# Batch tails in pairs, one more transpose by DMA, and a new order, in an attention and mixing kernel

## The chip, the cores and the metric

The kernel runs on one core of a Trainium2 chip. The metric is the device time of one launch in microseconds, the median of the runs. Engines are named as in the profile: PE multiplies matrices, PEld loads its weights, DVE is the vector engine, ACT the scalar engine, POOL the GpSimd engine, SP the engine whose queue issues every DMA here.

## The reference

There are 8 batches of 8 heads, 576 positions and 64 channels a head. Attention has a pooled part and a local part, and its result x (576 x 512 per batch) goes through a mixing layer:

```
out_d = softmax(q_d k_d^T / 8) v_d          # q, k, v averaged over groups of 4 positions
x = repeat(out_d, 4) + softmax(mask(q k^T / 8)) v   # mask: |i - j| < 4
theta = x @ w_theta
y = w_tok_r @ (x * cos(theta)) + w_tok_i @ (x * sin(theta))
u = x + y
out = u + max(u @ w_ch, 0)
```

## The kernel before, in words

The work of each batch is a set of generators, one for each kind of step, and each step puts a handful of instructions on the engines. One string, `ORDER` (L80), names the steps of all eight batches by letters, in the order in which they are issued. `pin` (L698) ties each instruction to the one before it on its engine, so that every engine follows this order strictly, and so does SP's queue of DMAs. A step that waits therefore holds up everything behind it on its engine. Data dependences between engines are semaphores.

The steps by letter: L and v load q, k and v; C and w cast them to bf16 (ACT for q of batch 0, otherwise POOL); A turns q and k (L324 to L343: PE transposes into PSUM, or for batches 6 and 7 DMA transposes issued by q at L296; ACT then copies in two halves, and DVE pools over four positions). B pools v (L350 to L359). Q makes the pooled scores and their exp (two steps, L382 to L409). S makes the local scores in five chunks with an exp on ACT (L438) and, but for batch 0, two band masks on POOL (L445, L447). N and V are the pooled and local outputs (L464, L502). T adds the two into x, transposed (L541, L545); for batches 6 and 7, t has turned it by DMA (L304) and POOL adds. H makes the angles and their cosine and sine (five steps, L562 to L580). Z multiplies them with x in the other layout: for batches 6 and 7 that comes from one DMA transpose (step x, L312), for the rest from PE (L604), 16 transposes a batch. X is the token mixing (L623 for 512 positions in four steps, L629 for the last 64, the tail), and DVE adds x (L624, L631). u turns u by DMA (L639 for the main part, L641 for the tail). R multiplies by w_ch (L653, and L661 for the tail), O adds on DVE (L675) and stores (L681, and L684 for the tail). W, c, l, g, h and D prepare weights and warm PE up.

S, N, Q and V, and the PE form of A, share two PSUM tiles of two banks, "w2", taken in turn. B, T, H, X, R, Z and the last step of N share four of one bank, "w1". The output tile `osb` has four buffers. ACT holds one table at a time: exp for Q and S, sine for H.

The tail of a batch has 64 positions. In R it fills both halves of the 128 partitions: at L661 eight matmuls of 256 columns, four for each half of the output channels, with the same 64 weights columns of u. In the store, the two halves go out as two DMAs of 64 KB in runs of 128 channels:

```
lhsT=uB[:, dc, :],
rhs=wch[:, dc, :].rearrange("p (j e d) -> p e j d", j=2, e=2)[:, hf],
```

Of the kernel before, what the change touches and what calls it, by code (L numbers as in the profile page):

```python
# [10 lines left out]
BF16 = mybir.dt.bfloat16  # L11
AF = mybir.ActivationFunctionType
ALU = mybir.AluOpType
AX = mybir.AxisListType

P = 128
B = 8
H = 8
S = 576
# [22 lines left out]
HALF = 64  # L42
MAIN = 512
# [4 lines left out]
def kernel(  # L48
# [11 lines left out]
    nc = tc.nc  # L60
# [5 lines left out]
    moep = ctx.enter_context(tc.tile_pool(name="moep", bufs=2))  # L66
# [9 lines left out]
    def w1(name, dt=FP32):  # L76
        return ps1.tile([P, 512 if dt == FP32 else 1024], dt, tag="w1" + next(turn1), name=name)


    ORDER = (  # L80
        "LKLLLLLKKCLCCAvCCLvCDwvvvKLCAACwwwwLASCLSVQQCBlLLLLLVSlllllNvlCCCCNlvvvACNVCcScwcvTlTTccllcwAASlHVVH"
        "wwwDTTcAHZHZcHSZcccSDDhLLLzBcCSCWQDVWWLghLLLLCWCCvQvWWLNCNCCWWSWvvLvZNVVXwwwvAAvhwhTXTAALXSwSLLLLXQQ"
        "TBCCVgLggHCuLLVTvHNTVHHZNCCHCCCSwzZZZARRvvvSwOROALSXOLLAAXLLwSwwLvCCCCSCCCCRSNVOXVVXQVTTTAABwSXuTLLA"
        "vvwuvQRvvLLSTSHONNHVLLXuZZANHCLwHwwLVVHRQRRCCCCOzvLLLBOOCCSSTZTCvvRwOTLZSQHVHNVTXTAAXLLACACwCHHwCLCq"
        "LwwqNVHXSZNVXZZvvzSLLCCQCLqXVZLqQvRvwBvOVTVuTTLXTAwASSCHCCHCHNNXqvLwwTwuVXLVLAAHHXqSSZXRQROzONZSCCQC"
        "TCZBSVqROqvvvvZTSSROTVHVRHOTNNTXAAHVHHVwwwwwXAtAXSSzXXSSZZNZVuRuuRRROOQQtOOBRVRVttROtTTTOZOSTNXVRTuN"
        "RRxSSOOOHHVVXtttVHZHZZHNVzZXXttXuXTTXXHTHTTRxROOZHHRuROOHZRZZzOXXXXXXXRuRRRuuOORRuOOROROOORROO"
    )

    staged = {}  # L90
# [86 lines left out]
    for i in range(2):  # L177
        t = const.tile([P, 4, 5, KP], BF16, name=f"kdP{i}")
# [4 lines left out]
    for i in range(2):  # L183
        t = const.tile([P, 4, 5 * 120], BF16, name=f"kT{i}")
# [4 lines left out]
    for i in range(2):  # L189
        t = const.tile([P, NCH, H, 66], BF16, name=f"v_w{i}")  # L190
# [4 lines left out]
    for c in range(NCH):  # L195
        t = const.tile([P, DM], BF16, name=f"tmp{c}")
# [4 lines left out]
    for i in range(2):  # L201
        t = const.tile([P, 2, H, 66], BF16, name=f"vd{i}")
# [12 lines left out]
    wch = wpool.tile([P, 4, DM], BF16, name="wch")  # L215
# [69 lines left out]
    parts, turned = {}, {}  # L285


    DMA_QK, DMA_X, DMA_Z = (6, 7), (6, 7), (6, 7)

    def turn_qk(b):  # L290

# [229 lines left out]
    def parted(t):  # L521

        return (t[:, 0:4 * MAIN].rearrange("p (e t) -> p e t", e=4),
                t[:, 4 * MAIN:4 * S].rearrange("p (e t) -> p e t", e=4))
# [85 lines left out]
            yield  # L610


    uTs, urs = {}, {}

    def mix(b):

        (xA, xB), z = parted(xTs[b]), zs.pop(b)
        uT = uTs[b] = moep.tile([P, 4 * S], BF16, tag="uT", name=f"uT{b}")
        uA, uB = parted(uT)
        for dc in range(4):  # L620
            ps = w1(f"psu{dc}_{b}")
            for j in range(9):
                nc.tensor.matmul(out=ps, lhsT=z[:, j, P * dc:P * dc + P], rhs=WT[:, j, 0:MAIN], start=(j == 0), stop=(j == 8))  # L623
            nc.vector.tensor_tensor(out=uA[:, dc, :], in0=ps, in1=xA[:, dc, :], op=ALU.add)  # L624
            yield
        ps = w1(f"psut_{b}")[:, 0:4 * HALF].rearrange("p (e t) -> p e t", e=4)
        for dc in range(4):
            for j in range(9):
                nc.tensor.matmul(out=ps[:, dc, :], lhsT=z[:, j, P * dc:P * dc + P], rhs=WT[:, j, MAIN:S],  # L629
                                 start=(j == 0), stop=(j == 8))  # L630
        nc.vector.tensor_tensor(out=uB, in0=ps, in1=xB, op=ALU.add)  # L631
        yield

    def u_turn(b):

        ur = moep.tile([P, 16, P], BF16, tag="ur", name=f"ur{b}")
        utr = moep.tile([P, 2, P], BF16, tag="utr", name=f"utr{b}")
        urs[b] = ur, utr
        nc.sync.dma_start_transpose(out=ur, in_=uTs[b][:, 0:4 * MAIN])  # L639
        yield  # L640
        nc.sync.dma_start_transpose(out=utr, in_=uTs[b][:, 4 * MAIN:4 * S])  # L641
        yield

    rels = {}

    def channels(b):

        uA, uB = parted(uTs[b])
        for c in range(5):
            psr = rels[b, c] = w1(f"psr{c}_{b}")  # L650
            if c < 4:
                for dc in range(4):
                    nc.tensor.matmul(  # L653
                        out=psr, lhsT=uA[:, dc, P * c:P * c + P], rhs=wch[:, dc, :],
                        start=(dc == 0), stop=(dc == 3),
                    )
            else:

                for dc in range(4):
                    for hf in range(2):  # L660
                        nc.tensor.matmul(  # L661
                            out=psr[64 * hf:64 * hf + 64, 0:256], lhsT=uB[:, dc, :],
                            rhs=wch[:, dc, :].rearrange("p (j e d) -> p e j d", j=2, e=2)[:, hf],
                            start=(dc == 0), stop=(dc == 3),
                        )
            yield

    def store(b):

        ur, utr = urs.pop(b)  # L670
        for c in range(5):
            psr = rels.pop((b, c))
            osb = moep.tile([P, DM], FP32, tag="osb", bufs=4, name=f"osb{c}_{b}")
            n = 4 if c < 4 else 2
            nc.vector.scalar_tensor_tensor(  # L675
                out=osb[:, 0:P * n].rearrange("p (e d) -> p e d", d=P),
                in0=psr[:, 0:P * n].rearrange("p (e d) -> p e d", d=P), scalar=0.0,
                in1=ur[:, c:16:4, :] if c < 4 else utr, op0=ALU.max, op1=ALU.add,
            )
            if c < 4:  # L680
                nc.sync.dma_start(out=out[b, P * c:P * c + P, :], in_=osb)  # L681
            else:
                for hf in range(2):
                    nc.sync.dma_start(  # L684
                        out=out[b, 512:576, :].rearrange("t (j e d) -> e t j d", j=2, e=2)[hf],
                        in_=osb[64 * hf:64 * hf + 64, 0:2 * P].rearrange("p (j d) -> p j d", j=2),
                    )
            yield

    last = {}
# [13 lines left out]
    def batches(steps):  # L709
        for b in range(B):  # L710
            yield from steps(b)

    sequences = dict(L=batches(load), v=batches(load_v), C=batches(cast), w=batches(cast_v), A=batches(turns), B=batches(pooled_v), Q=batches(scores), S=batches(band_scores), N=batches(pooled_out), q=batches(turn_qk), t=batches(turn_x), x=batches(turn_z),
                     V=batches(outputs), T=batches(transposes), H=batches(phases), Z=batches(modulate),
                     K=constants(), z=batches(z_turn), u=batches(u_turn), X=batches(mix), R=batches(channels), O=batches(store),
                     l=weight_loads(), c=weight_casts(), h=channel_loads(), g=channel_casts(), W=weight_turns(), D=warm_up())
    pin()
# [35 lines left out]
```

## Time and profile before

| what | before |
|---|---|
| median of 6 runs | 247.75 us (245.97 to 248.63) |
| the profiled execution, its time | 248.63 us |
| its span | 246.9 us |
| PE, DVE, ACT, POOL busy | 221.4, 185.8, 166.7, 161.4 us |
| mean granted clock of PE | 0.986 |
| L623, token mixing | 65.2 us of PE |
| L653 and L661, channel mixing, main and tail | 30.8 and 5.0 us of PE |
| L604, transposes of x | 96 matmuls |
| L675, tail additions | 8 of 417 ns |
| DMA issues L641, L684, L312 | 8, 16, 2 |

The span runs from the first to the last instruction; the time of an execution includes what lies around it. Busy times of an engine join overlapping instructions. A line of the page's fifth part gives the time of a group, the mean of one instruction, and how long the engine stood idle before them, with what ended the wait. The chain of waits follows back from the last instruction to what released each step. "L623" is line 623 of the kernel.

### The profile page before, as it was taken

How to read it: one execution, taken by the hardware profiler on the slowest of the kernel's cores; microseconds unless marked ns; L12 is line 12 of the kernel's file. 1: busy time of each engine (PE TensorE's matmuls, PEld its weight loads, DVE VectorE, ACT ScalarE, POOL GpSimd, SP SyncE). 2: the span in 40 equal slices, each digit the busy share in tenths (PEclk: the TensorE clock that was granted, in tenths of full speed). 3: DMA queues.
4: the chain of work that ended last, by engine and by line, in shares of the span. 5: the costliest groups of instructions: out<-in, count | busy, mean ns of one | idle time of the engine just before them, and what ended most of it. 6: DMA issues, size and time to landing. Idle time of an engine off the chain costs nothing. (4 is left out here: it accounts for less than half of the span.)

```text
span 246.9 us, 6575 instructions
## 1 busy us (share of the span) xinstructions
PE 221.4 (90%) x2569; PEld 134.1 (54%) x2602; DVE 185.8 (75%) x345; ACT 166.7 (68%) x248; POOL 161.4 (65%) x223
## 2 busy tenths in 40 slices
PE   0767799999999999999999998999699999999990
PEld 0434465765666566656666555655455655455540
DVE  5274979779879898887989977997787776256462
ACT  3586799766998479998878999899924390250000
POOL 4367466998999999989858764996295952400000
PEclk9999999999999999999999999999979999999997
DMA  6999999999999997999999999399869584957496
GB/s 197 302 252 377 314 188 322 316 231 231 317 229 286 310 213 137 281 249 295 234 202 214 264 196 269 50 195 201 120 155 156 138 210 93 169 182 87 91 262 202
DMA packets 100511, 53.94 MB, mean 218 GB/s; under 512 B 83968, under 2 KB 86016, under 8 KB 100480
## 3 DMA queue, kind: packets, MB, share of 16 engines
q1 hardware_dynamic: 100480, 53.53, 91.8%
q8 instruction: 20, 0.33, 0.6%
q14 instruction: 11, 0.09, 0.1%
HBM read 33.59 MB, written 9.44 MB: 174 GB/s over the span
## 5 line engine op out<-in xcount | busy, mean ns | idle before, releaser
L623 PE MATMUL psu<-WT,z 128*128 128x512 bf16 x273 | 65.2, 379 | 1.3 <-ACT cs L568 0.5
L445 POOL TENSOR_SCALAR_AFFINE_SELECT pm<-pm 128x1024 bf16<-128x1024 bf16 (+1 forms) x35 | 36.7, 1049 | 18.7 <-ACT pm L438 18.7
L438 ACT ACTIVATE pm<-psS 128x1024 bf16<-128x1024 f32 (+1 forms) x40 | 37.7, 979 | 11.6 <-PE psS L430 10.7
L623 PEld LDWEIGHTS <-z 128*128 128x128 bf16 x288 | 26.8, 98 | 29.2 <-issue 0.8
L447 POOL TENSOR_SCALAR_AFFINE_SELECT pm<-pm 128x1024 bf16<-128x1024 bf16 (+1 forms) x35 | 36.6, 1046 | 2.4
L624 DVE TENSOR_TENSOR uT<-psu,xT 128x512 bf16<-128x512 f32 x32 | 21.8, 686 | 12.8 <-PE psu L623 12.6
L562 PE MATMUL psth<-wth,xT 128*128 128x512 bf16 x120 | 30.9, 379 | 0.5
L653 PE MATMUL psr<-wch,uT 128*128 128x512 bf16 x119 | 30.8, 385 | 0.6 <-issue 0.2
L131 POOL CAST v_w<-st_v 128x512 bf16<-128x512 f32 (+1 forms) x40 | 24.0, 615 | 10.0 <-DMA st_v<-in_v_dram 10.0
L567 ACT ACTIVATE cs<-psth,pihc 128x512 bf16<-128x512 f32 x32 | 22.2, 695 | 11.8 <-PE psth L562 11.3
L511 DVE TENSOR_TENSOR tmp<-psloc,rl 120x512 bf16<-120x512 f32 (+2 forms) x40 | 27.6, 690 | 1.4
L342 DVE TENSOR_REDUCE qdT<-qT 128x288 bf16<-128x1152 bf16 x16 | 21.5, 1347 | 9.4 <-ACT qT L334 9.4
L675 DVE SCALAR_TENSOR_TENSOR osb<-psr,ur 128x512 f32<-128x512 f32 x32 | 21.5, 686 | 7.7 <-PE psr L653 6.7
L342 DVE TENSOR_REDUCE kdP<-kT 128x300 bf16<-128x1200 bf16 x16 | 22.3, 1396 | 5.5 <-ACT kT L334 5.5
L124 POOL CAST k_tm<-st_k 128x576 bf16<-128x576 f32 x32 | 21.7, 677 | 5.3 <-DMA st_k<-in_k_dram 4.8
L334 ACT COPY qT<-pstr 128x576 bf16<-128x576 bf16 x24 | 14.2, 646 | 9.2 <-PE pstr L332 9.2
L545 DVE TENSOR_TENSOR xT<-xTps,xdT 128x480 bf16<-128x480 bf16 (+3 forms) x36 | 18.7, 547 | 1.5 <-PE xTps L541 1.3
L124 POOL CAST q_tm<-st_q 128x576 bf16<-128x576 f32 x28 | 18.6, 664 | 1.6 <-PE pstr L332 1.0
L568 ACT ACTIVATE cs<-psth 128x512 bf16<-128x512 f32 x32 | 19.3, 604 | 0.0
L653 PEld LDWEIGHTS <-uT 128*128 128x128 bf16 x128 | 11.6, 99 | 12.5 <-issue 1.3
L430 PE MATMUL psS<-qT,kT 64*128 64x128 bf16 (+1 forms) x320 | 14.9, 217 | 3.2 <-ACT pm L438 2.2
L502 PEld LDWEIGHTS <-pm 128*128 128x128 bf16 (+1 forms) x320 | 14.8, 104 | 4.8 <-issue 0.5
(92 smaller groups left out, 389.1 us busy)
## 6 DMA issues: line engine op xcount, KB each, us to landing
st_q<-in_q_dram SPq DMA_DIRECT2D x32, 288.0 KB, 5.2
st_k<-in_k_dram SPq DMA_DIRECT2D x32, 288.0 KB, 4.9
st_v<-in_v_dram SPq DMA_DIRECT2D x32, 256.0 KB, 5.2
out_dram<-osb SPq DMA_DIRECT2D x32, 256.0 KB, 3.1
st_v<-in_v_dram SPq DMA_DIRECT2D x8, 192.0 KB, 4.9
tok<-in_moe_w_tok_r_dram SPq DMA_DIRECT2D x4, 288.0 KB, 7.2
tok<-in_moe_w_tok_i_dram SPq DMA_DIRECT2D x4, 288.0 KB, 5.3
th<-in_moe_w_theta_dram SPq DMA_DIRECT2D x2, 512.0 KB, 7.0
```

The costliest lines, as they stand in the source:

```text
L124: eng[i](out=dst[:, hh // 2, :, hh % 2, :], in_=staged.pop((b, f"{'qk'[i]}{hh}")).rearrange("p (r d) -> p r d", d=D))
L131: gp(out=v_ws[b % 2][0:KW[c], c, :, 0:D], in_=staged.pop((b, f"v{c}"))[0:KW[c], 0:DM].rearrange("p (h d) -> p h d", d=D))
L342: nc.vector.tensor_reduce(out=dst, in_=src, axis=AX.X, op=ALU.add)
L438: nc.scalar.activation(out=pv, in_=ps[0:kw].rearrange("p e (j w) -> p (e j) w", w=P)[:, :, 0:qn], func=AF.Exp, scale=SCL,)
L445: nc.gpsimd.affine_select(out=pv, in_=pv, compare_op=ALU.is_ge, fill=0.0, base=off, pattern=[[0, 8], [-1, qn]], channel_multiplier=1)
L447: nc.gpsimd.affine_select(out=pv, in_=pv, compare_op=ALU.is_ge, fill=0.0, base=6 - off, pattern=[[0, 8], [1, qn]], channel_multiplier=-1)
L511: nc.vector.tensor_tensor(out=tmp[0:cnt].rearrange("p (e j d) -> p e j d", e=2, j=4), in0=pv[0:cnt, :, :, 0:D], in1=rl[0:cnt].unsqueeze(3) ...
L562: nc.tensor.matmul(out=th, lhsT=xA[:, dc, P * c:P * c + P], rhs=wth[:, dc, :], start=(dc == 0), stop=(dc == 3),)
L567: nc.scalar.activation(out=cs[:, 0, :], in_=th, func=AF.Sin, bias=pihc, scale=1.0)
L623: nc.tensor.matmul(out=ps, lhsT=z[:, j, P * dc:P * dc + P], rhs=WT[:, j, 0:MAIN], start=(j == 0), stop=(j == 8))
L624: nc.vector.tensor_tensor(out=uA[:, dc, :], in0=ps, in1=xA[:, dc, :], op=ALU.add)
L653: nc.tensor.matmul(out=psr, lhsT=uA[:, dc, P * c:P * c + P], rhs=wch[:, dc, :], start=(dc == 0), stop=(dc == 3),)
```

## The change

Three things are changed. First, u of the tail is kept for two batches side by side (tile `uB`, one for each pair), so that R treats the 128 tail positions of a pair as one more chunk of four matmuls of 512 columns. This is done with the odd batch: an even batch now has four R and four O steps, an odd one five. The tails of a pair are turned by one DMA transpose of four blocks, added by one DVE instruction of 512 columns and stored by two DMAs of 64 rows of 2 KB. Second, batch 5 takes x for Z by a DMA transpose as batches 6 and 7 do. Third, `ORDER` is another string throughout; the tail's steps are fewer in it (O and R 36 for 40, u 12 for 16, x 3 for 2), and the other letters are as many as before.

The ends of the two strings, in the letters above (batch.step, from the last main mixing of batch 7 on):

```
before: X7.3 X7.4 R6.0 u6.0 R6.1 R6.2 R6.3 u6.1 u7.0 O6.0 O6.1 R6.4 R7.0 u7.1 O6.2 O6.3 R7.1 O6.4 R7.2 O7.0 O7.1 O7.2 R7.3 R7.4 O7.3 O7.4
after:  X7.3 R6.0 R6.1 R6.2 u7.0 R6.3 O6.0 O6.1 O6.2 O6.3 X7.4 u7.1 R7.0 R7.1 O7.0 R7.2 R7.3 O7.1 R7.4 O7.2 O7.3 O7.4
```

The stretch from the cosines of batch 5 on, without the steps that load or cast:

```
before: H5.0 V5.4 R2.4 H5.1 O2.4 T5.3 N6.0 N6.1 T5.4 X4.0 A7.0 A7.1 H5.2 V6.0 H5.3 H5.4 V6.1 X4.1 A7.2 t6.0 A7.3 X4.2 S6.3 S6.4 z5.0 X4.3 X4.4 S7.0
after:  H5.0 H5.1 N6.0 N6.1 T5.3 X4.0 T5.4 V6.0 V6.1 q7.3 A7.0 A7.1 x5.0 H5.2 H5.3 X4.1 A7.2 H5.4 A7.3 u3.0 S6.3 S6.4 X4.2 X4.3 z5.0 Z5.0 u3.1 R3.0 u4.0 Q7.0
```

The diff, without the string:

```diff
-    DMA_QK, DMA_X, DMA_Z = (6, 7), (6, 7), (6, 7)
+    DMA_QK, DMA_X, DMA_Z = (6,7),(6,7),(5,6,7)
...
-        uT = uTs[b] = moep.tile([P, 4 * S], BF16, tag="uT", name=f"uT{b}")
-        uA, uB = parted(uT)
+        uT = uTs[b] = moep.tile([P, 4 * MAIN], BF16, tag="uT", name=f"uT{b}")
+        uA = uT.rearrange("p (e t) -> p e t", e=4)
+        if b % 2 == 0:
+            uBs[b // 2] = moep.tile([P, 4, 2, HALF], BF16, tag="uB", name=f"uB{b // 2}")
+        uB = uBs[b // 2][:, :, b % 2, :]
...
-        nc.sync.dma_start_transpose(out=ur, in_=uTs[b][:, 0:4 * MAIN])
-        yield
-        nc.sync.dma_start_transpose(out=utr, in_=uTs[b][:, 4 * MAIN:4 * S])
-        yield
+        ur = urs[b] = moep.tile([P, 16, P], BF16, tag="ur", name=f"ur{b}")
+        nc.sync.dma_start_transpose(out=ur, in_=uTs[b])
+        yield
+        if b % 2:
+            utr = utrs[b // 2] = moep.tile([P, 4, P], BF16, tag="utr", name=f"utr{b // 2}")
+            nc.sync.dma_start_transpose(out=utr, in_=uBs[b // 2].rearrange("p e i t -> p (e i t)"))
+            yield
...
-        for c in range(5):
+        for c in range(4 + b % 2):
             psr = rels[b, c] = w1(f"psr{c}_{b}")
...
+            for dc in range(4):
+                nc.tensor.matmul(
+                    out=psr, lhsT=uA[:, dc, P * c:P * c + P] if c < 4 else uBs[b // 2][:, dc],
+                    rhs=wch[:, dc, :], start=(dc == 0), stop=(dc == 3),
+                )
             yield
...
             nc.vector.scalar_tensor_tensor(
-                out=osb[:, 0:P * n].rearrange("p (e d) -> p e d", d=P),
-                in0=psr[:, 0:P * n].rearrange("p (e d) -> p e d", d=P), scalar=0.0,
-                in1=ur[:, c:16:4, :] if c < 4 else utr, op0=ALU.max, op1=ALU.add,
+                out=osb.rearrange("p (e d) -> p e d", d=P),
+                in0=psr.rearrange("p (e d) -> p e d", d=P), scalar=0.0,
+                in1=ur[:, c:16:4, :] if c < 4 else utrs.pop(b // 2), op0=ALU.max, op1=ALU.add,
             )
...
-                for hf in range(2):
-                    nc.sync.dma_start(
-                        out=out[b, 512:576, :].rearrange("t (j e d) -> e t j d", j=2, e=2)[hf],
-                        in_=osb[64 * hf:64 * hf + 64, 0:2 * P].rearrange("p (j d) -> p j d", j=2),
-                    )
+                for i in range(2):
+                    nc.sync.dma_start(out=out[b - 1 + i, 512:576, :], in_=osb[HALF * i:HALF * i + HALF])
             yield
```

More of the change, by code (lines that the diff above doesn't have):

```diff
@@ L80 @@
     ORDER = (
[L81 to L87, printed above, removed]
+        "LLLLLLKCLLKvvvvCKCAvLLCCCKCCDAAwwwwALlSlLllLLwSSLlllQVLllBQVVNNvvCCCccCCACvvvCNlTTCcllLcASScccwHVVDT"
+        "TLLwATZcAHcwwwHHHZZScQLvLLLDDBQZCWSzLCcCcDvvvvVWWSWhNWWCCCLhhhLLLCCSWNWvWVAvXVANwwXLLAwAwwXSSXVBCQTT"
+        "TLLSTQCCHggggVHCCCVTHNNZuvHCCVLHzSZZLvRRLLOZOwwAAXAAXCwvvwSCCvvSCLLLLRvOROwSSXVVXAABQXCCwwQVCNTCLLLS"
+        "vTTSTTSuvvHNNHVXZZwLALAHVHVCwLwCCCHCNRQLLZzLRRLLLQuOOOvBvvvvvwSTSTTROZACCCVXSwHVNHTNTAXwAACvLHVLvCwC"
+        "HHwCSXVZXCSBVXVNQZZZzLLqLLQwCCTTCSSqwRLOqTTwwLLAqCCuVLLHCwXNCCHTVXVAqALqHNHHSXXAvBSSRROvzvCCZOZSCSXV"
+        "NZZSROqTQQTTRVVOHHNNTXTVVqwwwAAxHHXAHAuSSvwvXXzZwuRuQQRSSROOONVXSZBtttVTtRVZTZTtTRTOORSSXxVOXNRORVOH"
+        "VttROHNHHVZHXZZZzVNtXXXXTTXtHtTTTuxHRRROOHHuROOZHZRZZzOXXXuXXXRRRuROOOOXuRRORROROOO"
     )
@@ L610, in modulate @@
             yield
-    uTs, urs = {}, {}
+    uTs, uBs, urs, utrs = {}, {}, {}, {}
     def mix(b):
         (xA, xB), z = parted(xTs[b]), zs.pop(b)
-        uT = uTs[b] = moep.tile([P, 4 * S], BF16, tag="uT", name=f"uT{b}")
-        uA, uB = parted(uT)
+        uT = uTs[b] = moep.tile([P, 4 * MAIN], BF16, tag="uT", name=f"uT{b}")
[3 more added lines that the diff above has]
+        uB = uBs[b // 2][:, :, b % 2, :]
         for dc in range(4):
@@ L634, in u_turn @@
     def u_turn(b):
-        ur = moep.tile([P, 16, P], BF16, tag="ur", name=f"ur{b}")
-        utr = moep.tile([P, 2, P], BF16, tag="utr", name=f"utr{b}")
-        urs[b] = ur, utr
-        nc.sync.dma_start_transpose(out=ur, in_=uTs[b][:, 0:4 * MAIN])
+        ur = urs[b] = moep.tile([P, 16, P], BF16, tag="ur", name=f"ur{b}")
+        nc.sync.dma_start_transpose(out=ur, in_=uTs[b])
         yield
-        nc.sync.dma_start_transpose(out=utr, in_=uTs[b][:, 4 * MAIN:4 * S])
-        yield
+        if b % 2:
+            utr = utrs[b // 2] = moep.tile([P, 4, P], BF16, tag="utr", name=f"utr{b // 2}")
+            nc.sync.dma_start_transpose(out=utr, in_=uBs[b // 2].rearrange("p e i t -> p (e i t)"))
+            yield
@@ L644 @@
     rels = {}
     def channels(b):
-        uA, uB = parted(uTs[b])
-        for c in range(5):
+        uA = uTs[b].rearrange("p (e t) -> p e t", e=4)
+        for c in range(4 + b % 2):
             psr = rels[b, c] = w1(f"psr{c}_{b}")
[L651 to L655, printed above, removed]
-                    )
-            else:
-                for dc in range(4):
-                    for hf in range(2):
[L661 to L665, printed above, removed]
+            for dc in range(4):
[3 more added lines that the diff above has]
+                )
@@ L666, in channels @@
             yield
     def store(b):
-        ur, utr = urs.pop(b)
-        for c in range(5):
+        ur = urs.pop(b)
+        for c in range(4 + b % 2):
             psr = rels.pop((b, c))
             osb = moep.tile([P, DM], FP32, tag="osb", bufs=4, name=f"osb{c}_{b}")
-            n = 4 if c < 4 else 2
             nc.vector.scalar_tensor_tensor(
-                out=osb[:, 0:P * n].rearrange("p (e d) -> p e d", d=P),
-                in0=psr[:, 0:P * n].rearrange("p (e d) -> p e d", d=P), scalar=0.0,
-                in1=ur[:, c:16:4, :] if c < 4 else utr, op0=ALU.max, op1=ALU.add,
+                out=osb.rearrange("p (e d) -> p e d", d=P),
+                in0=psr.rearrange("p (e d) -> p e d", d=P), scalar=0.0,
+                in1=ur[:, c:16:4, :] if c < 4 else utrs.pop(b // 2), op0=ALU.max, op1=ALU.add,
@@ L682, in store @@
             else:
-                for hf in range(2):
-                    nc.sync.dma_start(
-                        out=out[b, 512:576, :].rearrange("t (j e d) -> e t j d", j=2, e=2)[hf],
-                        in_=osb[64 * hf:64 * hf + 64, 0:2 * P].rearrange("p (j d) -> p j d", j=2),
-                    )
+                for i in range(2):
+                    nc.sync.dma_start(out=out[b - 1 + i, 512:576, :], in_=osb[HALF * i:HALF * i + HALF])
             yield
```

## The prediction

> **What bounds the kernel now.** I read four views in this order: busy time and slices, stretches of 5 us, the chain of waits, and the groups of instructions. The page first:
>
> ```profile
> span 246.9 us, 6575 instructions
> PE 221.4 (90%) x2569; PEld 134.1 (54%) x2602; DVE 185.8 (75%) x345; ACT 166.7 (68%) x248; POOL 161.4 (65%) x223
> ...
> PE   0767799999999999999999998999699999999990
> ...
> PEclk9999999999999999999999999999979999999997
> ```
>
> PE is busy for 221.4 of 246.9 us. Its 25.5 us of idleness lie in the load at the start (slices 1 to 5), in one hole in slice 29, and in the last two slices. So PE work is worth its full time except where PE waits. The stretches around the hole:
>
> ```profile
> 170.00:175.00 5.00, 4.94 (x65) 2.81 (x65) 3.37 (x6) 4.98 (x7) 1.04 (x2) 1.00 0.91 143
> 175.00:180.00 5.00, 2.81 (x50) 2.53 (x47) 4.04 (x7) 4.99 (x6) 2.74 (x3) 0.84 0.72 149
> 180.00:185.00 5.00, 4.78 (x39) 2.20 (x37) 3.92 (x7) 0.26 (x2) 4.79 (x6) 0.82 0.50 136
> ```
>
> The columns are PE, PEld, DVE, ACT, POOL, granted clock, DMA share. From 170 to 180 ACT is full, PE loses 2.2 us, and the clock falls to 0.84 and 0.82. The wait, in the timeline of PE and ACT:
>
> ```profile
> 174.80 1.28 ACT L438 ACT_TABLE_LOAD   x1
> ...
> 176.10 3.52 ACT L438 ACTIVATE pm<-psS 128x1024 bf16<-128x1024 f32 x4
> 177.17 0.40 PE L430 MATMUL psS<-qT,kT 64*128 64x128 bf16 x8 [1.92 <-ACT pm L438]
> ```
>
> PE wants a two-bank PSUM tile (there are two, used in turn) that the first exp after the cosines of batch 5 must empty. The chain in order of time ends so:
>
> ```profile
> 234.81 3.59 DMA out_dram<-osb
> ...
> 240.29 2.25 DMA out_dram<-osb
> 242.54 0.03 issue
> 242.57 0.05 DVEq L675
> 242.62 0.04 issue
> 242.66 0.42 DVE osb L675
> ```
>
> At the end PE no longer decides: an addition waits for one of four output tiles (osb), which a store must release.
>
> **What the Trainium skill says.** "TensorE: Matmul & The Clock Gate", section Back-to-back issue gap: a warm matmul of N columns takes N/2.4 + 2.5 ns when isolated, 216 ns at 512. The trace agrees: eight of 512 columns took 1.73 us in the chain. The same page, section What's actually happening: the clock halves after an idle window of about 3.4 us and needs about as long a busy one to return. Here a hole of 1.92 us was enough for 0.84 and 0.82 over ten us, a loss of (0.16+0.18) x 5 = 1.7 us of clock. "ScalarE: Activation LUTs", section What ACT_TABLE_LOAD costs: 1283 ns for a change of table; the trace has 1.28 us. "DMA: Bandwidth & Descriptors", section Rules for kernel authors: join small transfers, since under 64 KB one pays mostly overhead; the trace agrees, 64 KB landed in 2.8 us and 256 KB in 3.1 us.
>
> **The change, part by part.** Sums are against the profiled execution: span 246.9 us, time 248.63 us, so 1.7 us lie outside. The median, 247.75 us, is 0.9 lower; I move it by the same difference.
>
> (1) Tails in pairs. A batch's tail is eight matmuls (L661), which run in twos; the pair of batches will take four of 512 columns, priced at the L653 row. From the chain in order of time (start us, us, what):
>
> ```profile
> 188.57 0.22 PE psxt L604 x4
> ...
> 215.07 1.73 PE psr L653 x8
> ...
> 220.71 0.56 PE psr L661 x8
> ```
>
> Eight tails cost 8 x 0.56 = 4.48 us, four joint ones 4 x 0.865 = 3.46: PE -1.02 us, of which 6 x 0.56 - 3 x 0.865 = 0.76 fall before the last main mixing of batch 7 (I call its end t0, 232.14 us). DVE: 8 x 0.417 becomes 4 x 0.686, -0.6 us, free of value while DVE is at 75%; the last addition, however, grows by 0.27 on the end path. SP: 16 tail issues of 0.59 become 8, priced at the main store's 0.38 to 0.59, and 8 transposes at L641 of 1.19 become 4. That frees over 9 us of a queue that is mostly waiting; taken as nothing, except at the end, below. An even batch's tail now waits for its odd neighbour. Only reserved tiles hold it, no engine; cost 0.
>
> (2) x of batch 5 by DMA. It removes 16 transposes at L604, 4 x 0.22 = 0.88 us of PE, all before t0. DVE's products at L605 cost 682 ns from either source: 0. It adds one transpose on SP (L312: 1.35 to 1.93 us to issue, 4.3 to land). It is placed behind the last qk transpose of batch 7 and ahead of the u transpose of batch 3. From its source (the addition at T5.4) to its first reader (Z5.0) PE has two cosine groups, the tail of cosines, two score chunks, two output chunks and three mixing chunks, about 9 us, over the 6.2 it needs: covered; uncovered it costs 0 to 1.9 us. The u transpose behind it (1.3 to 6.2 us to issue, 4.3 to 8.2 to land) is wanted some 11 us later. The DMA engines have room, at 0.72 of their time in the stretch of the hole. Below zero neither can go, since no work but PE's, already counted, is taken away.
>
> (3) New order. The work of ACT and POOL is unchanged, with as many table loads as before (14). I added up PE's steps in both orders: up to the first cosine step of batch 5 (H5.0) it has 138.0 us of work in either. From there to the matmul that needs the first exp:
>
> - before, to S7.0: cosines 4 x 0.865 + 0.47, three psloc of 0.25, one tail 0.56, two transposed chunks of 0.22, psnd 2 x 0.51, mixing 4 x 1.945 + 1.05, two score chunks of 0.27: 16.1 us;
> - after, to Q7.0: the same cosines, two psloc, no tail, mixing 4 x 1.945 only, the first R of batch 3 (0.865), else the same: 15.1 us.
>
> ACT's row over this stretch (table load, five cosine steps, four qk steps of two or more copies each, table load, first exp) runs from 159.73 to 177.1, 17.4 us without a gap, and is the same in both. So PE arrives 1.0 us earlier and waits 1.0 us longer: 2.9 instead of 1.92 us. That takes back 1.0 of the 1.64 us saved: t0 moves by -0.6. The unknown is how far ACT lags as H5.0 begins: in before it waited 0.56 us there, thus no lag. The bound is from 1.0 us lag less (the other waits for ACT in 140 to 155, 1.4 us, vanish) to 2 more. Value taken: none.
>
> Start: 7.9 of the 13.6 us idle in the first 40 us wait for the second q cast; its three loads and the engines' work for it keep their order. The other 5.7 us can move by the placing of batch 1's casts; POOL now does the pooled-v product first. Bound -1.5 to +1.5, taken as 0, since both orders have PE 28 to 29 us into its work when the token weights are turned.
>
> (4) The end. From t0 before: 246.9 - 232.14 = 14.8 us, last store issued at 243.7 = t0 + 11.6. After: R6.0-3 end at t0+3.46, X7.4 at 4.51, R7.0-3 at 7.97, the joint tail at 8.84. SP has the u transpose of batch 7 (issue 0.8 to 2.1), four stores, the joint tail's transpose at 5.0 to 6.2, landed by about 8.6 (covered by R7). The ring of four osb decides: O7.0 runs at 5.8 to 6.45, its store starts at 6.5 and lands in 3.1 (the median; 2.25 to 3.6 in the chain), 9.6. Then the tail's addition 0.69, two issues: the last at t0+10.75, against 11.6: -0.8 us (-1.5 by PE's bound with the fast landing, -0.3 with the slow).
>
> Sum: -0.6 - 0.8 = -1.4. The profile's 248.6 becomes 247.2, the median 247.75 becomes 246.3. The hole at the first exp of batch 6's last chunks is late next, then the osb ring.
>
> **Rivals.**
> A. PE's work counts in full, the hole doesn't grow, because ACT is given its earlier work sooner: -1.64 - 0.8 = -2.4, 245.3 us; with the hole and its clock loss gone, up to 3.9 less. For it: ACT is only 68% busy. Against: 17.4 us of ACT in a row facing 15.1 of PE.
> B. Slower: the hole passes the point at which the clock stays halved for a further stretch. If ACT lags by 1.5 us at H5.0, since Q6.0 and Q6.1 now come directly before it, the hole is 4.4 us, and a second loss like the 1.7 us seen follows: 246.3 + 1.5 + 1.7 = 249.5. It decides once the hole exceeds the page's window of 3.4 us. Against: from S6.0 to H5.0 ACT has 4.7 us of work to PE's 6.5.
> C. The start moves by its bound alone: 244.8 to 247.8.
>
> **Numbers.** Forecast 246.3, chance 0.42 (own range 245.3 to 247.3, so 0.22 on the faster side and 0.20 within 0.5%); A 0.28 (0.26 faster, 0.02 within); B 0.25, slower; C's upper end 0.05 (0.03 within, 0.02 slower). 0.5%, 1.2 us, is about what a measurement can tell from no change. Faster 0.48, same 0.25, slower 0.27. Range 243.3 (A with part of the hole gone) to 249.5 (B).
>
> **What would show it.** L604 with 80 matmuls, L653's line without a 256-column form, PE busy near 219.5; a wait of about 2.9 us for an exp, now before L382; clock at 0.8 there; last store issued about 0.8 us sooner after the last mixing. Wrong if PE's idle in the first 40 us differs from 13.6 by over 1.5, if the hole is below 1.5 or above 4, or if DVE waits for xr or ur.

## The result, and the profile after

The change makes the kernel slower, where a gain of 0.6% was forecast.

| what | before | after |
|---|---|---|
| median | 247.46 us (41 runs, 245.97 to 249.85) | 249.83 us (20 runs, 248.46 to 251.11) |
| ratio of the two | | 1.0093, 95% interval 1.0073 to 1.0113 |
| the profiled execution, its time | 248.63 us | 250.53 us |
| its span | 246.9 us | 248.7 us |
| mean granted clock | 0.986 | 0.981 |

Here and below a ratio is of the fast runs alone, while a median also counts the few runs over 1.5% above the fastest of their kernel.

The page of after, busy time and slices:

```profile
span 248.7 us, 6423 instructions
PE 220.5 (89%) x2502; PEld 132.7 (53%) x2538; DVE 186.2 (75%) x341; ACT 167.1 (67%) x248; POOL 162.7 (65%) x223
...
PE   0876899999999999999999798999499999999990
PEclk9999999999999999999999999999869999999997
```

PE has 64 weight loads fewer (2538 for 2602; 67 fewer records of matmuls), and is busy 0.9 us less, although more of its work ran at half clock: the saved work is there. But the hole in slice 29 is deeper (4 where it was 6), a shallower one has come in slice 23, and the clock is low in two slices of the forty, not one. The stretches around the hole (the columns are those shown for before):

```profile
170.00:175.00 5.00, 4.95 (x35) 2.29 (x30) 2.79 (x4) 5.00 (x9) 0.00 (x0) 1.00 0.93 183
175.00:180.00 5.00, 1.62 (x18) 0.80 (x18) 3.91 (x4) 4.97 (x6) 1.47 (x2) 0.79 0.28 55
180.00:185.00 5.00, 4.78 (x41) 2.46 (x41) 1.97 (x4) 2.52 (x4) 4.86 (x7) 0.53 0.86 209
```

PE works 1.62 us of the five from 175 on, against 2.81 before; and in the next five, in which it is busy almost throughout, the granted clock is 0.53, against 0.82. The timeline of ACT and PE gives the wait itself:

```profile
176.08 1.28 ACT L438 ACT_TABLE_LOAD   x1
177.37 1.69 ACT L438 ACTIVATE pm<-psS 128x1024 bf16<-128x1024 f32 x2
```

```profile
178.45 0.97 PE L382 MATMUL psSd<-qdT,kdP 64*128 64x144 bf16 x8 [3.25 <-ACT pm L438]
```

It is the wait of before, now at L382 and 3.25 us long. Before had one more short wait behind its 1.92 us:

```profile
177.84 0.40 PE L430 MATMUL psS<-qT,kT 64*128 64x128 bf16 x8 [0.27 <-ACT pm L438]
```

The clock records of the two traces show stretches at half the full clock, each 3.4 us long: before has one here, from 178.4; after has two, 6.8 us from 177.9. The chain of waits ends so:

```profile
233.56 2.60 PE psr L655 x12
...
236.26 3.56 DMA out_dram<-osb
...
239.94 0.70 DVE osb L667
...
240.67 3.36 DMA out_dram<-osb
...
244.16 0.69 DVE osb L667
```

In the new numbering L626 and L632 are the token mixing, L655 the channel mixing, L667 the addition and L673 its store. As before, the end hangs on the four output tiles: O7.0 waits for a store of batch 6, and the joint tail's addition for the store of O7.0.

**Where the time went, step by step.** In both traces I took each step's first weight load on PE and compared its time with the PE work of the steps ahead of it, by the prices of the prediction. The difference, counted from the first transposition of q, is the time that PE has lost by then:

| up to | lost before | lost after | difference |
|---|---|---|---|
| H5.0, cosines of batch 5 | 12.74 us | 15.95 us | +3.21 us |
| S6.3, late chunks of scores | 12.98 | 16.01 | +3.03 |
| R4.0, channel mixing of batch 4 | 17.30 | 22.44 | +5.14 |
| X7.3, last main mixing | 17.60 | 22.54 | +4.94 |

After began its transpositions 1.88 us sooner (6.00 against 7.88 us; in the traces below this start lies anywhere from 6.0 to 8.1 us, 6.0 to 7.7 in the new order and 6.4 to 8.1 in the old one), and it has 1.64 us less PE work ahead of t0. So t0 moves by 4.94 - 1.88 - 1.64 = +1.4 us (232.14 to 233.56), and the end behind it grows from 14.76 to 15.14: +0.4. That is the +1.8 of the spans. The two places to explain are the way to H5.0 and the way from S6.3 to R4.0, the hole.

### The profile page after: what moved, and what is told of

It is laid out like the page before. It is cut to its first block, busy times and chain, and to the rows that moved or that the text cites. A ratio compares the mean times of both kernels' runs of the same rounds, so it can differ in the third digit from the quotient of the medians.

```text
span 248.7 us, 6423 instructions
## 1 busy us (share of the span) xinstructions
PE 220.5 (89%) x2502; PEld 132.7 (53%) x2538; DVE 186.2 (75%) x341; ACT 167.1 (67%) x248; POOL 162.7 (65%) x223
## 4 chain that ended last, share of the span: by engine, by line
PE 66%; ACT 9%; POOL 8%; DMA 5%; SPq 4%; DVE 3%; issue 2%; DVEq 0%; POOLq 0%; ACTq 0%
PE psu L626 21%; PE psr L655 9%; PE psth L562 8%; PE psloc L502 4%; PE psS L430 4%; PE pstr L332 3%; PE psut L632 3%; DMA out_dram<-osb 3%; SPq L110 3%; ACT kT L334 2%; DMA st_v<-in_v_dram 2%; PE xTps L541 2%; PE wu L277 2%; ACT qT L334 2%; ACT pm L438 2%
## 5 line engine op out<-in xcount | busy, mean ns | idle before, releaser
L626 PE MATMUL psu<-WT,z 128*128 128x512 bf16 x275 | 65.0, 379 | 0.9 <-issue 0.3
L438 ACT ACTIVATE pm<-psS 128x1024 bf16<-128x1024 f32 (+1 forms) x40 | 37.6, 980 | 10.5 <-PE psS L430 9.1
L626 PEld LDWEIGHTS <-z 128*128 128x128 bf16 x288 | 26.7, 98 | 29.5 <-DVE z L605 0.2
L655 PE MATMUL psr<-wch,uT 128*128 128x512 bf16 x120 | 31.4, 393 | 0.4 <-issue 0.2
L667 DVE SCALAR_TENSOR_TENSOR osb<-psr,ur 128x512 f32<-128x512 f32 x32 | 21.4, 682 | 10.5 <-PE psr L655 7.9
L502 PEld LDWEIGHTS <-pm 128*128 128x128 bf16 (+1 forms) x320 | 14.8, 103 | 8.0 <-issue 1.1
L655 PEld LDWEIGHTS <-uT 128*128 128x128 bf16 x128 | 12.0, 100 | 13.1 <-issue 1.5
L545 DVE TENSOR_TENSOR xT<-xTps,xdT 128x480 bf16<-128x480 bf16 (+3 forms) x36 | 18.0, 547 | 0.2
L502 PE MATMUL psloc<-v_w,pm 128*128 128x65 bf16 (+1 forms) x320 | 16.9, 197 | 1.3 <-POOL v_w L131 0.8
```

The source lines that it names most:

```text
L438: nc.scalar.activation(out=pv, in_=ps[0:kw].rearrange("p e (j w) -> p (e j) w", w=P)[:, :, 0:qn], func=AF.Exp, scale=SCL,)
L502: nc.tensor.matmul(out=pv[0:qn, h // 4, h % 4, :], lhsT=pms[b][c][0:kw, 4 * par + blk, 0:qn], rhs=v_w[0:kw, c, h, 0:65], start=(h % 4 == 0 ...
L655: nc.tensor.matmul(out=psr, lhsT=uA[:, dc, P * c:P * c + P] if c < 4 else uBs[b // 2][:, dc], rhs=wch[:, dc, :], start=(dc == 0), stop=(dc ...
```

## The experiments

The theory after the result: the hole at the first exp, 3.25 us long, halves the clock for a second 3.4 us, which costs more than the change saves. Its rivals: the saved PE work lay beside other waits anyway; ACT reaches H5.0 late, because of the order; the joint tail lengthens the end. Ratios are to the kernel before, run beside each.

### Order and structure apart

`e1_old_order` has both structural parts in the order of before; `e2_new_order_only` has neither, in the new order.

```diff
 e1: after, ORDER of before without R, O .4 and u .1 of even batches
+    ... T5.4 x5.0 X4.0 ...
 e2: before, ORDER of after without x5.0; even batches get their R, O .4 and u .1 back
+    ... O2.3 R2.4 O2.4 H5.0 ...
```

> The joint tails and the transpose of batch 5 by DMA, in the order of before (the tail's steps of even batches left out, the new transpose behind T5.4). Theory H, the loss of 2.4 us lies in the new order, which opens a hole at the cosines of batch 4 and widens the one at the first exp of batch 6's last chunks: 246.0 us, the 1.9 us of PE work less about 0.5 that the old hole takes back. Rival J, the joint tail and the extra transpose cost it themselves, by the later u transposes and the busier DMA engines: 249 or more.

> The kernel of before in the new order (tails of even batches put back behind the last store of their batch, x of batch 5 on PE). H: slower than after, 250.5 us, since the order's holes stay and 1.9 us of PE work come back, part of which fills holes. J: about 247.5 us, as before.

Measured: e1 248.21 us, 1.0007 (0.9988 to 1.0026); e2 254.33 us, 1.0218 (1.0159 to 1.0276). The order alone costs 2.2% (by six runs of e2). The structure gains 1.2% in the new order and nothing in the old one. The loss is thus the order's, and the forecast's 1.64 us of saved PE work is worth nothing in the order of before.

`e9_z5_alone` and `e10_pairs_alone` split the structure in the old order (x of batch 5 by DMA; joint tails), and `e8_x5_on_pe` takes the DMA turn out of after.

```diff
 e9: before
-DMA_Z = (6, 7)
+DMA_Z = (5, 6, 7)
+    ... T5.4 x5.0 X4.0 ...
 e10: e1 without x5.0; e8: after without x5.0, and in both
-DMA_Z = (5,6,7)
+DMA_Z = (6,7)
```

> The kernel of before, with one part of the change: x of batch 5 by DMA, issued behind T5.4, order otherwise as before. Theory H (PE work counts, off the path little): 247.2 us, 0.9 less than before, all of it behind the second hole. Rival: the transpose gets in the way of the qk transposes and the u transpose in the queue and the time stays at 248.1 or rises.

> The kernel of before with the joint tails alone, in its own order. H: 248.1 to 248.3 us, nothing gained: the traces of the two together show PE's saved matmuls come back as waits ahead of H2.0 and S4.0, where PE waited for others anyway, and the end no shorter. Rival: 247.2, the 1.0 us of PE work.

> The changed kernel with x of batch 5 turned by PE again (the transpose at L312 for batch 5 left out). If the DMA transpose is free: 0.9 us of PE come back behind the second hole, 250.5 us. If it delays the queue and the u transpose behind it: 249.5 or less.

Measured: e9 247.98 us, 1.0007 (0.9991 to 1.0024); e10 248.02 us, 0.9999 (0.9977 to 1.0021); e8 252.34 us, 1.0166 (1.0119 to 1.0213). Neither part is worth anything in the old order, while in the new one the DMA turn is worth 0.7% (by six runs of e8). In the old order the 0.88 us of transposes come back as waits. Behind the hole e9 has two that before doesn't have, as the list of PE's waits shows (engine, tile and line, what it waited for; total, times, longest, in us):

```profile
PE psloc L502 <- DVE tmp L511: 0.6, 1, 0.6
...
PE psr L661 <- DVE osb L675: 0.4, 1, 0.4
```

With a tail gone ahead of H2.0, the time lost between X0.0 and H2.0 rises by 0.6 us in e1 and e10: PE came earlier and waited. In the new order it is the other way round: with x of batch 5 on PE, e2 and e8 have a wait of the channel mixing for DVE's addition that after doesn't have, first the line of e2, then that of e8.

```profile
PE psr L653 <- DVE osb L675: 1.8, 1, 1.8
```

```profile
PE psr L655 <- DVE osb L667: 1.5, 1, 1.5
```

So the 2.2% of e2 are not the clock's alone: its profiled execution has no stretch of half clock behind the hole at all.

### The two waits on the way

`e3_a6_later` moves the step behind which the cosines of batch 4 wait (the shallow hole, slice 23: PE waited 1.52 us at L541 in after, and 0.2 us there in e6 and e13, which share its order up to that place, so most of it is chance). `e4_q7_later` puts four steps with work for PE ahead of Q7.0, where the deep hole is. `e5_h5_first` lets ACT have the cosines of batch 5 sooner.

```diff
 e3: after
-    ... L7.3 L7.4 A6.0 q6.3 ... V4.4 L7.5 L7.6 H4.0 ... H4.1 T4.4 V5.0
+    ... L7.3 L7.4 q6.3 ... V4.4 L7.5 L7.6 H4.0 ... H4.1 T4.4 A6.0 V5.0
 e4: after
-    u4.0 Q7.0 Q7.1 R3.1 S7.0 S7.1 R3.2 O3.0 O3.1 O3.2 N6.2 V6.2 X4.4
+    u4.0 R3.1 R3.2 O3.0 X4.4 Q7.0 Q7.1 S7.0 S7.1 O3.1 O3.2 N6.2 V6.2
 e5: after
-    R2.2 O2.2 q7.2 T5.0 Q6.0 Q6.1 T5.1 T5.2 R2.3 V5.3 V5.4 O2.3 H5.0
+    q7.2 T5.0 Q6.0 Q6.1 T5.1 H5.0 R2.2 O2.2 T5.2 R2.3 V5.3 V5.4 O2.3
```

> The changed kernel with one step moved: the first turn of batch 6 (A6.0) from ahead of V4.4 to behind T4.4. H: DVE no longer waits for that turn's DMA transpose ahead of the last output chunk of batch 4, the wait of 1.5 us at L541 goes; ACT does the same work later, so part comes back at the second hole: 248.5 to 249.3 us. J: 249.8, no change.

> The changed kernel with Q7.0 and Q7.1 moved behind R3.1, R3.2, O3.0 and X4.4, 2.8 us of PE work ahead of the matmul that waits for the exp. H: the hole of 3.3 us falls to about 0.5, the half clock's windows go from two to one or none: 246.5 to 247.5 us. Rival, the wait only moves to S7.0, since ACT stays behind: 249.5.

> The changed kernel with R2.2, O2.2, T5.2, R2.3, V5.3, V5.4 and O2.3 moved from ahead of the first cosine step of batch 5 (H5.0) to just behind it. Theory A: the second hole is set by the time at which ACT gets H5.0, since 17 us of ACT work without a gap follow; ACT waited 1.8 us for PE there, so the first exp and all behind it come 1.5 us sooner and a window of half clock may go: 246.5 to 248.5 us. Rival P: PE's late arrival there is only a sum of earlier waits and the moved work is missed later: 249.8 us.

Measured: e3 251.43 us, 1.0141 (1.0096 to 1.0185), e4 251.04 us, 1.0126 (1.008 to 1.0173), e5 249.09 us, 1.0045 (1.002 to 1.007). So e3 made things worse: in its trace 2.2 us of wait for DVE stand at an output of the pooled part. e4 didn't gain: the wait for the exp goes, and another comes in its place, in the list of PE's waits:

```profile
PE psr L655 <- DVE uT L627: 2.1, 1, 2.1
```

The channel mixing of batch 3 now comes before its input has been added, and two stretches at half clock are still there. Moving PE work in front of a hole fails when that work's own input is late. e5 wins back half of the loss by its ratio, though its runs spread from 247.3 to 251.8 us. So H5.0 is late, and some 0.5% hangs on it: the timeline of ACT has, ahead of those cosines, first in before, then in after,

```profile
159.73 1.28 ACT L567 ACT_TABLE_LOAD   x1 [0.56 <-issue]
```

```profile
161.06 1.28 ACT L567 ACT_TABLE_LOAD   x1 [1.75 <-issue]
```

that is 1.75 us of standing, against 0.56. The profile names no releaser, but PE reaches the first angles of H5.0 only at 159.92, behind R2.2, R2.3, V5.3 and V5.4, and the table load follows 0.3 us behind those 0.87 us of work.

`e11_best` tried the moves that these readings suggested in the order of before: e1 with seven output tiles, the cosines of batch 5 earlier, and channel mixing of batch 3 in the hole.

```diff
 e11: e1 with osb bufs=7, and
+    S6.2 H5.0 ... z5.0 u3.0 X4.3 X4.4 R3.0 R3.1 S7.0 S7.1 ... R3.2 O3.0 R3.3
```

> Joint tails, transpose of batch 5 by DMA, the order of before, seven output tiles, and two moves that follow from the holes: H5.0 directly behind S6.2, and R3.0, R3.1 (with their u transpose and store) ahead of S7.0. If ACT's row from H5.0 on and the PE work ahead of S7.0 set the second hole: 0.6 us sooner at H5.0, 1.7 us of work into the hole of 2.2, the half clock with it: 245 us. If the saved wait only moves: 247.5.

Measured: 249.8 us, 1.0087 (1.005 to 1.0123): a miss. Its longest waits are new ones:

```profile
PE psr L655 <- DVE osb L667: 2.4, 1, 2.4
PE psth L562 <- DVE xT L545: 1.5, 2, 1.0
```

R3.1 takes a PSUM tile that DVE hasn't emptied, and H5.0 is so early that it waits for its x. In an order that is tied this tightly, my step-by-step reading did not suffice to improve it by moving useful work.

### The clock behind the hole

If the loss is the clock, PE need not do useful work in the hole; any work will do. `e13_warm_in_hole` puts idle matmuls there: step D, six matmuls of 512 columns on constants, whose results are not used. `e16_warm_at_end` has the same twelve matmuls at a place where PE has no wait near, as a control. `e14_before_osb7_warm` and `e15_old_order_osb7_warm` do it for before and for e1, with seven output tiles.

```diff
 e13: after
-    u3.1 R3.0 u4.0 Q7.0
+    u3.1 D D R3.0 u4.0 Q7.0
 e16: after
+    D D X7.0
 e14, e15: before and e1, osb bufs=7
-    X4.4 S7.0
+    X4.4 D S7.0
```

> The changed kernel with twelve idle matmuls of 512 columns (two more warm-up steps, 2.6 us of PE at full clock, results not used) ahead of R3.0, in front of the hole at Q7.0. Theory K (half clock): the hole is as long, but PE is not idle in it, so the windows of half clock behind it go from two to none or one: 247.0 to 248.5 us. Rival N (the clock is a side issue): 249.8 us; if PE bounds there: 252.4.

> The changed kernel with the same twelve idle matmuls ahead of X7.0, where PE has no wait for 25 us: the control for the first of this call. PE work counts in full there: 252.4 us. If it doesn't, 250.

> The kernel of before with seven output tiles and six idle matmuls (1.3 us of PE) ahead of S7.0, in front of its hole of 1.9 us. K: the window of half clock, 1.7 us, goes in most runs: 245.5 to 246.5 us, against 247.0 with seven tiles alone. N: 247.0.

> Joint tails, transpose of batch 5 by DMA, the order of before, seven output tiles, and six idle matmuls ahead of S7.0. K: 246 us, against 247.7 without them. N: 247.7.

Measured: e13 247.73 us, 0.9998 (0.9977 to 1.0019); e16 251.9 us, 1.0169 (1.0127 to 1.0212); e14 245.64 us, 0.9905 (0.9872 to 0.9937, of only 7 runs); e15 246.54 us, 0.9952 (0.9936 to 0.9969). Twelve matmuls without use take away the whole loss of the change. At another place they cost 0.8% (1.0169 against 1.0093), some 1.9 us; they are 2.6 us of PE work, which the intervals allow. The stretches of e13:

```profile
175.00:180.00 5.00, 3.72 (x31) 1.58 (x30) 3.87 (x5) 4.53 (x6) 1.28 (x2) 1.00 0.27 52
180.00:185.00 5.00, 5.00 (x100) 3.30 (x99) 3.93 (x8) 4.05 (x6) 4.93 (x6) 1.00 1.20 226
```

The clock is 1.00 in both. (It was half for 6.8 us from 21.0 in this execution, in the start, so that its mean over the whole, 0.979, is no higher than that of after.) The idle matmuls in the timeline, and what remains of the wait:

```profile
174.30 2.75 PE L277 MATMUL wu<-warm,ident 128*128 128x512 bf16 x12
178.33 1.02 PE L655 MATMUL psr<-wch,uT 128*128 128x512 bf16 x4 [1.28 <-DVE uT L627]
```

Across traces, the time that PE lost from S6.3 to R4.0 beyond the work of the steps there (idle matmuls counted as loss) goes with the stretches of half clock; e4 and e5, which move steps across these marks, and e11 are left out:

| order | kernel | lost | half clock there |
|---|---|---|---|
| new | after, e6 | 6.4, 6.5 us | 6.8, 6.8 us |
| new | e3, e16 | 5.4, 5.2 | 3.4 each |
| new | e8 | 7.3, with 1.5 of the wait for DVE | 3.4 |
| new | e2 | 6.0, with 1.8 of the wait for DVE | none |
| new, idle matmuls in the hole | e13, e17 | 4.3, 4.2 | none |
| old | before, e1, e7 | 4.3, 4.6, 4.8 | 3.4 each |
| old | e9, e10, e12 | 3.8, 3.2, 2.7 | none |
| old, idle matmuls in the hole | e14, e15, e18 | 2.7, 4.2, 3.2 | none |

For the losses of e13 and e17, 2.6 us are the idle matmuls themselves; of the others with idle matmuls 1.3. Without the wait for DVE, e8 has 5.8 us and e2 4.2, so in the new order a hole of 3.0 to 3.3 us costs 4.2 us with no stretch, 5.2 to 5.8 with one and 6.4 to 6.5 with two. From Q7.0 to R4.0 alone, the same steps on PE, after needs 10.5 us from the end of the wait and e13 7.6: 2.9 us apart. Of the 6.8 us at half clock 0.55 lie in the wait and 6.25 behind it, and half of these is 3.1 us, which fits.

A profile is one execution. Over the runs that the ratios use, the mean granted clock tells how long a kernel ran at half clock, start and end included: 7.9 us in after, 5.1 in before (218 runs beside the experiments), 5.8 in e13. Counted at half its length, the difference between after and before is 1.4 us of the 2.4 measured, so the theory holds for a part of the loss. The idle matmuls took away 2.1 us of half clock in e13 against after, 2.6 in e14 against e12 and 4.8 in e15 against e7, which would be 1.1, 1.3 and 2.4 us of time; by the ratios they brought 2.4, 1.6 and 0.8. The sums agree, 4.7 us each before rounding; the pairs don't, so the size of the effect is known in the mean only.

**Where the hole lies seems to matter too.** In each of the twenty traces the times between two changes of the clock are whole multiples of 3.41 us: the changes lie on a grid, whose place differs from trace to trace. In the order of before, holes of nearly one length ended in two ways:

| trace | hole, us | borders of the grid at the hole | half clock |
|---|---|---|---|
| before | 175.25 to 177.17 | 175.0, 178.4 | from 178.4 |
| e1 | 175.53 to 177.27 | 174.3, 177.7 | from 177.7 |
| e7 | 175.69 to 177.35 | 174.7, 178.2 | from 178.2 |
| e9 | 174.87 to 176.79 | 176.0 | none |
| e10 | 175.69 to 177.31 | 176.6 | none |
| e12 | 174.77 to 176.68 | 175.7 | none |

A hole that lay whole between two borders was followed by a step of half clock, and one that a border divided was not. In after and e6 the hole ran 0.5 us past the border at which the clock fell, and a second step followed; in e3, e8 and e16 it had ended before that border, and there was one. The hole of e2 lay 2.0 us before a border and 1.0 us behind it. This was read from the traces afterwards, no run was made for it, and it doesn't cover all: in e4 and e5 steps with 1.1 and 1.3 us of small waits were followed by half clock, while a step of after with 1.4 us (at 136.9) was not.

### The end

`e6_osb7`, `e7_old_order_osb7` and `e12_before_osb7` give the output tiles seven buffers, in after, e1 and before.

```diff
-osb = moep.tile([P, DM], FP32, tag="osb", bufs=4, name=f"osb{c}_{b}")
+osb = moep.tile([P, DM], FP32, tag="osb", bufs=7, name=f"osb{c}_{b}")
```

> The changed kernel with seven output tiles (osb) for four. Theory R: the end is set by the ring of four, two landings of 3.4 and 3.6 us in a row; with seven the last addition waits for PE alone, 1.5 us sooner: 248.3 us. Rival S: the SP queue and the landing set the end anyway: 249.5 us.

> The joint tails and the transpose of batch 5 by DMA in the order of before, and seven output tiles. Theory R: 246.5 us, 1.2 less than before, since the PE work that is saved is no longer lost at the ring. Rival S: 247.7, as with four.

> The kernel of before with seven output tiles for four, nothing else. If its end is set by the ring, as its chain of waits says: 247.3 us, 0.8 less. If by the queue and the landing of the last store: 248.1, no change.

Measured: e6 249.69 us, 1.0068 (1.0047 to 1.009); e7 247.71 us, 0.9985 (0.9966 to 1.0004); e12 246.95 us, 0.9968 (0.995 to 0.9985). Each is 0.2 to 0.3% below the same kernel with four, which only e12 shows clear of noise by itself. So the ring of output tiles does hold the end, but not with all that the chain shows for it. In e6 the next thing is late, in the timeline of DVE:

```profile
243.50 0.69 DVE L667 SCALAR_TENSOR_TENSOR osb<-psr,utr 128x512 f32<-128x512 f32 x1 [1.50 <-DMA utr<-uB]
```

The last addition waits for the joint tail's transpose, which SP could issue only at 239.43, behind the burst of stores of batch 6.

`e17_new_order_mended` joins what helped in the new order: the idle matmuls, seven tiles, and the tail's mixing and transpose ahead of those stores. `e18_pairs_osb7_warm` asks whether joint tails alone are worth anything in the old order, once the hole is filled.

```diff
 e17: e13 with osb bufs=7, and at the end
-    X7.3 R6.0 R6.1 R6.2 u7.0 R6.3 O6.0 O6.1 O6.2 O6.3 X7.4 u7.1 R7.0
+    X7.3 X7.4 R6.0 R6.1 R6.2 u7.0 u7.1 R6.3 O6.0 O6.1 O6.2 O6.3 R7.0
 e18: e10 with osb bufs=7, and
-    X4.4 S7.0
+    X4.4 D S7.0
```

> The changed kernel with 12 idle matmuls of 512 columns ahead of R3.0 (their result is not used), seven output tiles instead of four, and at the end X7.4 directly behind X7.3 and u7.1 behind u7.0. Theory (the loss is the clock behind the hole, +1.7 us at least, and the end is held by the ring of four output tiles and then by the late transpose of the tail): the idle matmuls bring the 2 us that they brought alone, and the two mends of the end add about 1 us: 0.993 to 0.996 of the kernel before, some 246 to 246.8 us. Rival (the end is held by PE and by the landing of the last stores whatever the ring): no better than with the idle matmuls alone, 0.998 to 1.002.

> The kernel before, in its own order, with joint tails, seven output tiles and 6 idle matmuls of 512 columns ahead of S7.0 (their result is not used); x of batch 5 stays on PE. Theory (with the hole kept warm, PE work saved elsewhere still gives little in the old order, since PE waits for others there, but the joint tail's four R steps of the last batches are on the path): equal to or up to 0.3% better than the kernel before with seven tiles and idle matmuls, that is 0.987 to 0.991. Rival (joint tails cost at the end, since the tail's addition is longer and comes last): 0.993 to 0.996, like the old order with both parts of the change, seven tiles and idle matmuls, which gave 0.995.

Measured: e17 246.71 us, 0.9952 (0.9931 to 0.9974), as the theory had it; e18 247.35 us, 0.996 (0.9942 to 0.9978), in the size that the rival named, though hardly at the end, where it looked. In e17 the last step of the chain follows PE at once,

```profile
231.57 7.78 PE psr L655 x36
239.38 0.69 DVE osb L667
```

and the end is 14.1 us from the last main mixing, against 14.9 in e13 and 15.1 in after. In e18 the joint tails are worse than the separate ones of e14 (0.9905), although PE has less to do. In the profiles 1.0 us of the 2.1 between the two lie in the start, 0.9 arise up to the last main mixing, 0.6 of them where POOL's transposed x of batch 6 comes late, and 0.2 at the end. Why the joint tails should bring that lateness about isn't settled, and with 7 runs of e14 part of the difference may be chance; without idle matmuls e7 and e12 lie only 0.2% apart, and their intervals overlap.

The fastest kernel is thus before itself with seven output tiles and six idle matmuls in the hole: 245.64 us, 1.0% below before.

## Why the prediction was wrong, by its steps

**What bounds the kernel: half right.** The hole at the first exp and the output tiles were the two places named, and they are the two that count. But "PE work is worth its full time except where PE waits" was then used as if PE waited in the hole alone. It waits in small ones all along: PE loses 3.4 us from H2.0 to H5.0 in before, and in the order of before saved work ahead of a wait lengthened that wait (H2.0 in e1 and e10, L502 and L661 in e9).

**(1) and (2), 1.64 us of PE saved before t0: right in size, and its worth hangs on the order.** The work did go: 80 transposes of x, and no form of 256 columns in the channel mixing. In the order of before it is worth nothing (e1, e9, e10). In the new one, after against e2, the structure is worth 1.2%, some 3 us and so not less than its time, and this step is not what made the kernel slower. The addition at L605 and the transpose's own landing cost nothing, as said, and DVE waited for neither xr nor ur on the way.

**(3) the hole: right in mechanism, near in size, and its price left out.** 2.9 us were forecast and 3.25 measured. But the hole was costed as its own length only, and the clock behind it was put at nothing. Rival B had the missing term, a second loss of clock "like the 1.7 us seen", and tied it to a hole above 3.4 us. After 3.25 us it was there in after, and in e6; of the four other traces with this hole, three (e3, e8, e16) have one stretch as before, and e2 has none. By the stretches of 5 us the clock took (0.21 + 0.47) x 5 = 3.4 us in after against 1.7. From S6.3 to R4.0 PE lost 2.1 us more than before, of which 1.1 is the wait (3.25 against 1.92 and 0.27) and the rest fits the second stretch. With idle matmuls in the hole (e13) the kernel is level with before.

**(3) H5.0, "the unknown is how far ACT lags ... value taken: none": ACT didn't lag, PE came late.** ACT stood idle for 1.75 us there, more than the 0.56 of before. What failed is what the step took for granted, that both orders bring PE to H5.0 at one time because it has "138.0 us of work in either". PE came 1.3 us later by the clock (158.60 to 159.92), in spite of a start 1.9 us sooner: the same work in another order met other waits. In the traces of the new order without the shallow hole H5.0 has lost 14.3 to 15.4 us, in those of the old one 12.7 to 14.1; so some 1 us comes with the order, and another 1.3 in after's profile with the shallow hole. Moving seven steps behind H5.0 gained 0.5% (e5). Which of the order's other differences makes the 1 us is not shown. ACT then works from there to the first exp without a gap, as the step said, and so hands the delay on to the hole.

**(3) the start: within its bound of -1.5 to +1.5 us.** With the first mixing (X0.0) PE had lost 13.8 us in before and 12.6 in after, -1.2 us. The first transposition came 1.88 us sooner, and its time varies among executions.

**(4) the end, -0.8 us: measured +0.4.** The joint tail's addition, put at t0+9.6, came at t0+10.60; the addition behind the ring had been at t0+10.52 in before. Of the 1.0 us, 0.6 is O7.0 and its store (its addition at t0+6.38, its store at t0+7.11, where 6.5 was put, since batch 6's stores stood behind the u transpose on SP and the first landed in 3.56 us), 0.3 is its landing, 3.36 us where the median of before, 3.1, was put, and 0.1 lies between landing and addition. Thus the addition starts 0.1 us later than before instead of 0.9 sooner, and is 0.27 us longer, which the step had counted: +0.4.

**The sum.** -0.6 - 0.8 became +1.4 + 0.4. The range missed by 0.3 us. Rival B came nearest, with 249.5 us, rightly by its clock and otherwise by luck: ACT didn't lag and the hole wasn't 4.4 us long, while PE's lateness and the longer end, which B didn't have, made up for it. Of the signs that were to show the prediction wrong none came (PE's idle time in the first 40 us is 12.2 us, the hole 3.25, DVE waits for neither xr nor ur): they watched the length of the hole and not the clock behind it. Where the sum says "-1.4" and the chances 0.42 for it, the profile already had the warning: a hole of 1.92 us had cost 1.7 us of clock, so lengthening it should have been priced with the clock in it: with one more such loss, the forecast's -1.4 is +0.3 already.

The Trainium skill's page "TensorE: Matmul & The Clock Gate", section What's actually happening, says of the warming up that the window is free-running and that the point of change depends on where in it a matmul lands. The runs agree, and for the fall of the clock too: with holes of 1.6 to 1.9 us in the order of before, the half-clock stretch shows in three of six traces, as they lie on the grid. Its figure for the idle time needed, about 3.4 us, is longer than these holes; here the measurement decides.

## What to carry to other kernels

Price a wait of PE by its length and by the clock behind it, look at the granted clock in the stretches after each hole, and where useful work can't be moved in, try a few idle matmuls in the wait: here they brought 0.3 to 1.0% in three kernels, and cost 0.8% at the one other place tried. PE work that is removed can come back as a wait further on, in one order and not in another; test each saving in the old order, and the new order without the saving, before the two are joined. At the end of a kernel, follow the ring of output tiles and the order of issues on SP with the slowest landing in the chain, not with the median.

## What the runs showed of the hardware

The half clock came in units of 3.4 us on a grid of this step. Behind the hole at the first exp, 1.6 to 3.3 us long, there were none, one or two of them; they began between 0.55 us before PE resumed (after, 177.9 against 178.45) and 1.2 us behind it (before, 178.4 against 177.17). It is thus paid by the work behind the wait. In e2, whose hole is 3.0 us, no such stretch came: a hole of this length makes it likely, not sure. In the start, from 19 to 28 us, seven traces have one or two such units as well. Among 218 runs of before, those with a mean granted clock of 0.998 or more have a median of 247.0 us, those with 0.991 to 0.994 one of 247.6, with 0.985 to 0.988 248.5, and with 0.979 248.9; each further unit thus goes with 0.5 to 0.8 us, less than the 1.7 that half of its length makes. The start of the first transposition moved between 6.0 and 8.1 us among executions of nearly the same loads, nearly as much as the whole effect of the change.
